# Block-sparse attention and gated FFN on one core: q turned 128 columns at a time, in a re-made order

## The chip, the core and the metric

One core of a Trainium2 chip runs the whole program. The metric is device microseconds of one execution. The engines named here are PE (TensorE: matmuls and transposes), DVE (VectorE), ACT (ScalarE), POOL (GpSimd, which here mostly issues loads that cast to bf16) and SP (SyncE, which issues the other transfers). PE writes to PSUM alone; DVE and ACT copy results from PSUM to SBUF.

## The reference

Two layers follow each other: attention with a block mask, then a feed-forward layer with a gate made by a convolution of three taps.

```python
def _attn_ref(q, k, v, sampled_blocks):          # 4 batches, 8 heads, 768 tokens, 64 wide
    ...
    scores = scale * np.matmul(q, k.transpose(0, 1, 3, 2))
    ...
    mask = np.abs(blk_i - blk_j) <= window        # blocks of 32 tokens
    mask = mask | (blk_i == 0) | (blk_j == 0) | (blk_i == n_blocks - 1) | (blk_j == n_blocks - 1)
    for qb in range(n_blocks):
        for kb in sampled_blocks[qb]:
            mask[qb * block:(qb + 1) * block, kb * block:(kb + 1) * block] = True
    ...
    return np.matmul(attn, v).astype(np.float32)  # attn: softmax over the masked scores

def _moe_ref(x, w_in, conv_w, w_out):             # 512 -> 1024 -> 512
    h = np.maximum(x @ w_in, 0.0)
    ...
    for k in range(K):
        conv_out += conv_w[k][None, None, :] * hp[:, k:k + S, :]
    gate = 1.0 / (1.0 + np.exp(-conv_out))
    return (h * gate @ w_out).astype(np.float32)
```

## The kernel before, in words

The 32 heads are taken as 16 pairs. For each pair, q and k are brought to a layout with the 64 channels on partitions: tiles `e` and `o` (five slots of each) hold the even and the odd chunks of 128 tokens, for two heads, in rows 0 to 63. Rows 64 to 87 hold the mask: on the k side a pattern of the 24 blocks, on the q side 0 or -8000 for each block, so that one matmul over 88 rows gives masked scores.

Pairs 0 to 5 are turned on PE (`kq_transposes`, from line 427), pairs 6 to 15 by transposing transfers on SP (`kq_crossbar`). For a pair on PE, `k_tr` turns k by six transposes of 128 columns into a PSUM bank `mix`, and two copies take it to `e` and `o`. q comes in two halves of 384 tokens (`g` = 0 and 1): `q_tr` (line 504) turns each half by six transposes whose weights are 64 columns wide, one for each head and chunk, into rows 0 to 63 of a `mix` bank; two `q_cp` copies, one of both heads' two chunks of one parity (512 elements) and one of the rest (256), take it on. Pair 0's first half is done head by head from fp32 loads.

The scores are made in 144 units of eight 128x128 blocks (line 742, tile `st`, two tiles of two PSUM banks each). One `exp` of 128x1024 on ACT (line 753) turns a unit into `pt` (six buffers); eight `av` matmuls of 65 columns (line 775) multiply it with v and a column of ones. When its units are done, a segment of 384 tokens is normalised (`xtok`, DVE), turned (`xT`), multiplied with `w_in` (line 864, `f1`), passed through a relu on DVE or ACT (`hE`), convolved and gated on DVE with a tanh on ACT, and multiplied with `w_out` (line 802, `f2`). Each 128 tokens of output are copied from PSUM to an `o2s` buffer (`ev`) and stored by SP (`out`). There are eight halves of a batch; the last is cut into 256 and 128 tokens, so that the end is short. The two outputs of the last segment are collected in halves of an `st` tile instead of `mix` (`tail=True`).

In the head, PE runs matmuls on a zeroed tile `warm` while the first loads land. The q side of the mask comes from six small matmuls (`w24`) on the sampled blocks into one `st` tile, three for `e` and three for `o`; two copies (`m_q0`, `m_q1`) take it to rows 64 to 87 of slot 0, and further copies spread it to the other head and slots.

Every operation is first recorded with its inputs and buffers, and then put down in the order that the string `ORDER` gives: two characters for the operation, one for the engine where there is a choice (`V` DVE, `A` ACT), and one for each buffer that it takes. Each engine works through its own instructions in that order; waits between engines are added from the tiles that instructions share. So `ORDER` decides which engine makes a copy, which buffer it takes and what stands ahead of it.

Of the kernel before, what the change touches and what calls it, by code (L numbers as in the profile page):

```python
# [20 lines left out]
000m010g0f0n0h02030410o0i0t050p0j0q0s060zA1t00k0r070AA0l081u18A1090v1F00a0b1aA0c1H20d0N0w01bA19V1c00O0xA1i11f0  # L21
1dV00yA0e1jV1l11eV1kA1gA0R1o00E4K11hA4L0D4P01nA1mV1B14Q4M01v10u0Q0P1I1wV14R14U11xV4V1T11y00G4W24Z01V34+1zV0F1AA
1W5214/30H532521p11sV05445b02715c1qV1C00I1rA4N0125g15d55h1DV4O4S1J14r1GV1281EV5i04T4X1KV25l05m134Y1LV1M05n15q14s
1NV5r1450511OV555s25610K5z05A5e0J5f5j5B35E15705F1UV20U14t1X0582j05G45J00V5K1YV31+15L51ZV5k5o5O15P1/V5p5t20V5u5Q0
5T00T5v15U26V35C05D5w5H5V16010Y614u5I155M115N6225R6500M660B05S6730C6a16b0L5W5X1636c4646f05Y26g5Z591685x06h55aV0
6o15yV6p690Z6d6e6q05+16t04v1P05/V6i6j6u6k06y16l6v14w6z160+6m06r06s6A26nV6D00S6E0X4xhW12l06F3hZ00/6I16JhX4y2m6K4
h+hYV06R06Sh/Vi316T5i4ii06W14z176Xik6wi5Ai00iji16Y04A2x11Q1i2V6/0701RAil4B6x2116B7417111SV6C75iq1290im6G762ic1
2aV47d0idir7ein7i14C2bV2z26H7j7f36L6M1is2c04DieV6U6V6Z7k46+7n06N12eV7oit2217p5722dV7s17t24V2n023V7u0737x0iu7y2q1
2oV02B02A7z1777G16O7H784E2pV2F27g0iv7h7L07926P0io4F7l2H37M7I27a7m7q7rip07v7w7A7N37B16QV17Q12rV7R7J0W7K7b07S47V0
7C07W2kV47O2sV7X57D2C4G82183107P7E17T8407cV8707FV887Uiw7Y8918c1ix2J12I7Z8d2yV0i602GV18e28h04H7+12N08i7/i7i918j3  # L30
# [12 lines left out]
lW2bZculYcn1c40lB3zlXc5c9calFVcv33Hcy03I2czb+2lUcelZlCAmg03PlVcA4cD1cfcEl+mh3Mb/cF2cjcI0ck3uV1ma1c0m23l/cJcom3
cp1cQ1cRcK5m4cw3CcxcBm5cCcGmbcS0m0m6cV0cHcLm1cM3NcWm7c+1cq1micrcX1c/m8mccscN0m9cT0cUd03d30cOd4mjcPd54cY3Zmd3+2
mkV1d81d9meV0mm03Q0da5dg03DV2mn3JV2mo3EV423OcZmfdhd1mpdi03W3Gdl1mqV3dmmy1dn1mz3/mB0mC3X0mAA0dq0mDVd2drms1mW0ds2
mtmX3Rdv1dwmYmudx3mZmE0mv40m+431d6d7mwV2mFm/dD0dbmGVdEdI1dc1n0dF4mH1n10mIdJdd2mJAmN04cde4d3dN0dK5mOn21df2dj41dO
n3dkmK1n4dP0mL494a1n5domxdpdS1dTmPVmMA4hdtdudX0dU13SV3dYdy3TVmQ1mRdZ2n6e314e4i0e4na2dzmT0nbe53mUmSVdG0e80dHe9n7
mVVdLed1dA1eeni3ea4nw1dBdMdQdRncdVef5dCdWd+ei04fndejnq0n8ek0e00eq1neer3Fd/1n9e6e744es1ev0njewnrnkex3eA1e1eb3VeB
ecnlege2nfehel4gem3YV3et0eF0nmeC4nx4ong4p2eueyen2eznheGnneK1eonyeH5eLepnonsnpeDeEeM045V4eS0eT4jnteU2eX1nuV0eYnz
eZ14bV4eI48eJnAV2eNf00mrf1eO1eP1f5146Vf23mlf6nC0eQ47nDf74nI1eR0nEVnJfd04qV0nKAfe4kV1nL0ff5nM3Ufi1nNVnvfjnF14lV  # L50
fk0eV4nnGo60eWnBfn0fonHAo8nR0fp2nSo7fs1n+1e+e/ftnTAn/nO1fu1nPo9fx0o0fyf3nQAf4o1nU0fz3fF1oafGf8f9o2nVfH4nX1oe2fg0
fK0offLo3nYogfhfP1fa0fM5flnZVfQfmfqo4frfbobfU0o5fvfcfVnWAohoA1fR0ocfwou0om3fAodfW2g01g1onfB1fIovoig21g50oog6oBop
ojfJfNfC2fOoqfSg73fTga1fDgbfXfYokfEg30org4g8olg9gj0gkgc4osoCotowgl5fZ1go1f+gpoxgq0f/gdoDoyV3gt0gugeoM0gv24mgf0oN
ggozoOoEA1oPoFgC1oQA0gDgh1gH0giA1gIoS0gE1oToV1oUV1gJ3oWgM1oXVgNp20gO4p3pe1p51pgp6p4Apfgm1gV0p7AgngrphoY0oZpigW
o+Agso/1pu0pjp0pwoG0pvp1Ag+1g/gX5oHpm2oIpnh00oJpogwh30pph4oKA2gxpxpb1h52gF0pqoLpcp80gy2pkoRgGpdAgKgzgLgPhc1prpy
hdgQpl1gY1gZhe1h1p9psh2gR1h6ptgA1hh0paAh7gShigBAhq1h80pC3hrhj3pK0pDgT1pLh9hs4gUVhf0hz0pFhgha1hkpzhl1hbVhApEhthu
pZ1hB5hv2pGp+hwhE1pHp/VhFhN0hC1hOpAhG0q31pIpBq4pJhDpMq5Aqe1hHpNhP2hJ1hm0pQ1qfhnpRpOA3qhpSqu2ho0qgpThpA2qwhI0pW0
pUA1hKqvpXpVqihL1hQhRpYAhMVpPhS0hx1hThyAq60qjhU0q01hVVq7qR0qSq8q1qTAq9qkq2AqO0qaqPqlr31qbqX1qQVqYr4qcq+0qZAqU0qd
qVq/qm3qC1qWAqor01qDqnr50qI0r1r6r80r2rd1qpri0qqr9rer7ro1qrqxrprf1qyra0qJqsqzqtrjqEqAqBqKrbqLrcrgqFrhqMA2rqqGV0qN
rrrkqHrsA1rlrtrmA3rn  # L60
# [22 lines left out]
class Graph:  # L83
# [29 lines left out]
def kernel(  # L113
# [11 lines left out]
    nc = tc.nc  # L125
# [51 lines left out]
    warm = sb.tile([128, 512], BF16, tag="warm", name="warm")  # L177
# [20 lines left out]
    def t_act(n):  # L198
        return 0.055 + n / 1200.0
# [12 lines left out]
    def T(u):  # L212
        return T0 + PACE0 * u if u < 18 else T0 + 18 * PACE0 + PACE1 * (u - 18)

    SW = 0.715
    NWARM = 11
# [4 lines left out]
    o_imem = op("ident_mem", {"DVE": 0.1}, lambda e: nc.vector.memset(ident, 0.0), -20)  # L221
    o_warm = op("warm_mem", {"DVE": 0.3}, lambda e: nc.vector.memset(warm, 0.0), -20, after=[o_imem])
    o_amem = op("a_mem", {"DVE": 0.1}, lambda e: nc.vector.memset(A, 0.0), -18, after=[o_warm])
# [4 lines left out]
    for x in range(NWARM):  # L228
        def warm_mm(e, n=512 if x < 6 else 256):
            nc.tensor.matmul(out=av_t[b_warm.index][:, 0:n], lhsT=warm[:, 0:128], rhs=warm[:, 0:n], start=True, stop=True)  # L230
        prev = op("warm", {"PE": 0.215 if x < 6 else 0.108}, warm_mm, -20 + 0.2 * x, [o_warm], after=[prev],
                  alloc=[b_warm] if x == 0 else [], uses=[] if x == 0 else [b_warm])
# [92 lines left out]
    m_q = [op("m_q0", {"ACT": 0.45, "DVE": 0.55}, q_rows(E_t[0], 0), -17, [o_w], uses=[b_w]),  # L325
           op("m_q1", {"DVE": 0.55, "ACT": 0.45}, q_rows(O_t[0], 1), -17, [o_w], uses=[b_w])]
# [96 lines left out]
    def kq_transposes(P):  # L423
# [70 lines left out]
        def q_half(g, src, ldq, nbuf, pr, hs=(0, 1)):  # L494
# [11 lines left out]
            if P == 0 and g == 1:  # L506
                pr = T(14)
# [22 lines left out]
        for hs in ([0], [1]) if P == 0 else ([0, 1],):  # L530
            q_half(0, lambda: nat_t[nb.index][:, 0, 0:384].rearrange("p (h c) -> p h c", h=2),
                   ld_q[hs[0]:hs[0] + 1] if P == 0 else ld_q, nb,
                   -16 + 2.1 * hs[0] if P == 0 else due - 3, hs)
# [6 lines left out]
        q_half(1, lambda: nq_t[nq.index], [lq1], nq, due1 - 4)  # L540
# [252 lines left out]
    def out_block(b, t, due, deps, after, tail=False):  # L793
# [13 lines left out]
        evo = op("ev", {"ACT": t_act(512), "DVE": t_dps(512) + 0.06}, lambda e: dcopy(e, o2s_t[ob.index], acc()),  # L807
                 due + 2.5, [prev], alloc=[ob], uses=[mb])
        op("out", {"SP": 0.6}, lambda e: nc.sync.dma_start(out=out[b, 128 * t:128 * t + 128, :], in_=o2s_t[ob.index]),
           due + 3, [evo], uses=[ob], dma=("hw", 0.65))  # L810
# [207 lines left out]
```

## Time and profile before

| | |
|---|---|
| time, median of 3 runs | 216.37 us (215.73 to 220.55) |
| span of the profiled execution | 213.9 us (the page gives no time beside it) |
| PE busy | 203.6 us, 95% |
| ACT busy | 193.5 us, 90% |
| DVE busy | 186.6 us, 87% |
| POOL busy | 60.4 us, 28% |
| granted TensorE clock | 1.000 |
| exps on ACT | 144, 1027 ns each |
| loads and stores | 24.81 MB, mean 116 GB/s |

The span goes from the first to the last instruction; the times of the runs include what lies around it. Matmuls overlap in PE's pipeline, so a busy share of 95% is not 95% of PE's peak: the distance from one start to the next is what a matmul costs in a dense stretch. The first exp starts at 7.88 us, and the last instruction before the final store ends at 210.9 us.

### The profile page before, as it was taken

Reading aid. Unit: us, or ns where it says so; the run is one execution under the profiler, and the core shown is the slowest. Engines: PE = TensorE matmul, PEld = TensorE weight load, DVE = VectorE, ACT = ScalarE, POOL = GpSimd, SP = SyncE. Lnnn points to the kernel's source line nnn. Section 1 sums busy time; section 2 is a strip of 40 time slices with the busy share of each in tenths; the row PEclk is TensorE's granted clock in tenths of the full one; section 3 lists DMA queues with packets and bytes.
Section 4 is the critical chain, followed back from the end, with each engine's and each line's share of the span. In section 5 each row is a group of like instructions: output and inputs, shape, how many; then the busy total and the mean of one; then the engine's idle time right before and its main releaser. Section 6 shows DMA issues by size and latency. Waiting matters only on the chain.

```text
span 213.9 us, 6829 instructions
## 1 busy us (share of the span) xinstructions
PE 203.6 (95%) x2702; PEld 154.0 (72%) x2721; DVE 186.6 (87%) x577; ACT 193.5 (90%) x252; POOL 60.4 (28%) x117
## 2 busy tenths in 40 slices
PE   7899999999999999999999999999998999999991
PEld 3679978887677775778776766787786867785740
DVE  4899989999989994999999978999799939999980
ACT  6999999999899997999999977999999988997642
POOL 8883455733323130500327152730000000000000
PEclk9999999999999999999999999999999999999999
DMA  6999898998888977693599869699941130200205
GB/s 181 186 195 202 132 123 119 113 172 99 99 123 99 138 133 162 122 106 74 103 234 96 116 104 188 105 143 114 134 154 23 20 122 3 98 5 21 80 0 196
DMA packets 48935, 24.81 MB, mean 116 GB/s; under 512 B 35120, under 2 KB 45832, under 8 KB 48904
## 3 DMA queue, kind: packets, MB, share of 16 engines
q0 software_dynamic: 19728, 11.05, 43.0%
q1 hardware_dynamic: 28888, 13.05, 30.0%
q8 instruction: 21, 0.34, 0.7%
q10 hardware_dynamic: 288, 0.30, 0.4%
q14 instruction: 10, 0.08, 0.1%
HBM read 23.08 MB, written 6.29 MB: 137 GB/s over the span
## 4 chain that ended last, share of the span: by engine, by line
PE 66%; DVE 24%; ACT 6%; issue 3%; ACTq 0%; DVEq 0%
PE st L742 19%; PE mix L802 16%; PE mix L864 12%; PE av L775 10%; DVE m L916 9%; ACT pt L753 4%; DVE m L924 4%; DVE hE L886 3%; PE st L802 2%; PE mix L504 2%; PE av L230 2%; DVE xtok L694 1%; DVE gT L971 1%; DVE o L340 1%; DVE e L340 1%
## 5 line engine op out<-in xcount | busy, mean ns | idle before, releaser
L753 ACT ACTIVATE pt<-st 128x1024 bf16<-128x1024 f32 x144 | 141.3, 1027 | 5.6 <-PE st L742 4.2
L775 PE MATMUL av<-vt,pt 128*128 128x65 bf16 x1152 | 60.4, 193 | 0.2
L775 PEld LDWEIGHTS <-pt 128*128 128x128 bf16 x1152 | 52.3, 97 | 10.1
L864 PE MATMUL mix<-xT,winb 128*128 128x384 bf16 (+2 forms) x288 | 52.8, 308 | 0.3 <-DVE hE L886 0.3
L916 DVE TENSOR_SCALAR m<-hE,cw 128x382 bf16<-128x382 bf16 (+2 forms) x192 | 49.4, 320 | 0.2
L802 PE MATMUL mix<-woutb,gT 128*128 128x512 bf16 x157 | 44.6, 379 | 1.6 <-DVE gT L971 0.6
L742 PE MATMUL st<-o 88*128 88x128 bf16 (+1 forms) x240 | 44.5, 229 | 0.3 <-ACT pt L753 0.2
L742 PE MATMUL st<-o,e 88*128 88x128 bf16 (+1 forms) x228 | 44.2, 233 | 0.2 <-ACT pt L753 0.2
L742 PE MATMUL st<-e,o 88*128 88x128 bf16 (+1 forms) x224 | 42.5, 234 | 1.2 <-ACT pt L753 1.1
L742 PE MATMUL st<-e 88*128 88x128 bf16 (+1 forms) x208 | 41.8, 239 | 0.4 <-ACT pt L753 0.2
L742 PEld LDWEIGHTS <-o 88*128 88x128 bf16 x464 | 34.3, 97 | 8.9 <-issue 2.0
L742 PEld LDWEIGHTS <-e 88*128 88x128 bf16 x436 | 32.9, 97 | 9.0 <-issue 0.9
L924 DVE TENSOR_TENSOR m<-m 128x764 bf16<-128x764 bf16 (+2 forms) x64 | 33.8, 533 | 0.3
L864 PEld LDWEIGHTS <-winb 128*128 128x128 bf16 x288 | 24.2, 97 | 8.2 <-issue 0.8
L963 ACT ACTIVATE m<-m 128x764 bf16<-128x764 bf16 (+2 forms) x32 | 26.3, 821 | 1.9 <-DVE m L924 1.8
L414 POOL COPY pace<-pt 1x1 bf16<-1x1 bf16 x24 | 7.6, 315 | 58.9 <-ACT pt L753 58.8
L802 PEld LDWEIGHTS <-gT 128*128 128x128 bf16 x192 | 15.7, 97 | 11.7 <-DVE gT L971 2.3
L886 DVE TENSOR_SCALAR hE<-mix 128x384 bf16<-128x384 f32 (+2 forms) x30 | 16.4, 553 | 7.9 <-PE mix L864 7.6
L884 ACT ACTIVATE hE<-mix 128x384 bf16<-128x384 f32 (+2 forms) x34 | 16.5, 492 | 3.1 <-PE mix L864 2.2
L971 DVE TENSOR_TENSOR gT<-m,hE 128x764 bf16<-128x764 bf16 (+3 forms) x36 | 18.3, 511 | 0.5
L694 DVE TENSOR_TENSOR xtok<-av,rcp 128x384 bf16<-128x384 f32 (+2 forms) x36 | 18.2, 507 | 0.4
L239 POOL DMA_DIRECT2D nat<-in_q_dram x23 | 16.9, 734 | 2.4 <-issue 1.9
(88 smaller groups left out, 170.0 us busy)
## 6 DMA issues: line engine op xcount, KB each, us to landing
out_dram<-o2s SPq DMA_DIRECT2D x24, 256.0 KB, 2.6
nat<-in_k_dram POOLq DMA_DIRECT2D x15, 192.0 KB, 4.0
vn<-in_v_dram POOLq DMA_DIRECT2D x15, 192.0 KB, 5.5
nat<-in_q_dram POOLq DMA_DIRECT2D x6, 192.0 KB, 4.2
winb<-in_moe_w_in_dram POOLq DMA_DIRECT2D x2, 512.0 KB, 8.4
woutb<-in_moe_w_out_dram POOLq DMA_DIRECT2D x4, 256.0 KB, 4.8
nat<-in_q_dram POOLq DMA_DIRECT2D x9, 96.0 KB, 5.4
nq<-in_q_dram POOLq DMA_DIRECT2D x6, 96.0 KB, 4.5
```

Of the source, the lines that this page charges most:

```text
L239: return op(name, {eng: occ}, lambda e: on(e).dma_start(out=dst(), in_=src), prio, deps, dma=(kind, service), **kw)
L694: nm = op("norm", {"DVE": t_dps(128 * C)}, lambda e: nc.vector.tensor_tensor(out=xtok_t[xk.index][:, 0:C].rearrange("p c h d -> p h c d"), ...
L742: nc.tensor.matmul(out=st[:, 128 * x:128 * (x + n_)], lhsT=QK[kc % 2][s][0:88, 1, hh, kc // 2, :], rhs=QK[par][s][0:88, 0, hh, idx:idx + n ...
L753: nc.scalar.activation(out=pt_t[ptb.index], in_=st_t[stb.index], func=AF.Exp, bias=0.0, scale=0.125)
L775: nc.tensor.matmul(out=o[:, off:off + 65], lhsT=pt_t[ptb.index][:, 128 * x:128 * x + 128], rhs=V_t[vslot_b[P].index][:, hh, kc, 0:65], sta ...
L802: nc.tensor.matmul(out=acc(), lhsT=gT_t[gb.index][:, ffc, 128 * t:128 * t + 128], rhs=woutb[:, ffc, :], start=(ffc == 0), stop=(ffc == NFF ...
L864: nc.tensor.matmul(out=mix_t[hb.index][:, w1 * y:w1 * y + w1], lhsT=winb[:, fc, 128 * ffc:128 * ffc + 128], rhs=xT_t[xt_buf[n].index][:, f ...
L886: nc.vector.tensor_scalar(out=dst, in0=src, scalar1=0.5, scalar2=0.0, op0=ALU.mult, op1=ALU.max)
L916: nc.vector.tensor_scalar(out=m_t[cb.index][:, x, y, 0:w], in0=hE_t[heb.index][:, f0 + y, t0 + x:t0 + x + w], scalar1=cw[:, x, f0 + y:f0 + ...
L924: nc.vector.tensor_tensor(out=m[:, a_, :, 0:w], in0=m[:, a_, :, 0:w], in1=m[:, b_, :, 0:w], op=ALU.add)
L963: th = [op("tanh", {"ACT": t_act(2 * w) + 0.04}, lambda e, cb=cb, w=w: nc.scalar.activation(out=m_t[cb.index][:, 0, :, 0:w], in_=m_t[cb.in ...
L971: nc.vector.tensor_tensor(out=gT_t[gtb.index][:, f0:f0 + 2, t0:t1], in0=m_t[cb.index][:, 0, :, 0:w], in1=hE_t[heb.index][:, f0:f0 + 2, 1 + ...
```

## The change

Five things are changed.

- For all halves of q on PE except pair 0's first, a new function `q_half` turns 128 columns at a time: the 384 columns of a partition are two heads of three chunks of 64, so that three transposes of 128 columns leave one chunk in rows 0 to 63 and the next in rows 64 to 127. Four copies, each of one head and one parity, of 256, 128, 256 and 128 elements, take them to `e` and `o`. The old function stays as `q_head` for pair 0's first half.
- `w24` becomes two operations of three matmuls each, and each mask copy names only its own.
- The tile `warm` has 256 columns, not 512, and is set to zero before `ident`. There are 14 warm matmuls of 256 columns (six of 512 and five of 256 before) and 14 more of 128, the fillers, which `ORDER` places among the first units.
- In the last segment's outputs, `ev` is two copies of 256 columns, not one of 512; `ORDER` puts the first on DVE and the second on ACT for the two outputs that use `st`.
- `ORDER` is another string, so that the place, the engine and the buffer of operations differ all over the kernel.

```diff
-    for x in range(NWARM):
-        def warm_mm(e, n=512 if x < 6 else 256):
+    for x in range(NWARM + NFILL):
+        def warm_mm(e, n=256 if x < NWARM else 128):
             nc.tensor.matmul(out=av_t[b_warm.index][:, 0:n], lhsT=warm[:, 0:128], rhs=warm[:, 0:n], start=True, stop=True)
...
-    def w24(e):
-        w = st_t[b_w.index]
-        for x, chunks in enumerate((ECH, OCH)):
+    o_w = []
+    for x, chunks in enumerate((ECH, OCH)):
+        def w24(e, x=x, chunks=chunks):
+            w = st_t[b_w.index]
             for y, (g, c) in enumerate(chunks):
...
-    o_w = op("w24", {"PE": 0.34}, w24, -17, [o_a4, o_nblk], alloc=[b_w])
+        o_w.append(op("w24", {"PE": 0.33}, w24, -17, [o_a4, o_nblk] + o_w, alloc=[] if x else [b_w], uses=[b_w] if x else []))
...
+        def q_half(g, src, ldq, nbuf, pr):
+            mb = Buf(P_mix)
+
+            def fn(e):
+                t = mix_t[mb.index].bitcast(BF16)
+                for y in range(3):
+                    nc.tensor.transpose(out=t[:, 128 * y:128 * y + 128], in_=src()[:, 128 * y:128 * y + 128], identity=ident)
...
+            X, Y = (E_t, O_t) if g == 0 else (O_t, E_t)
+            for hh, t, at, n_, p0, c0 in ((0, X, g, 2, 0, 0), (0, Y, 2 * g, 1, 64, 0), (1, X, g, 2, 64, 128), (1, Y, 2 * g, 1, 0, 256)):
+                def cp(e, hh=hh, t=t, at=at, n_=n_, p0=p0, c0=c0):
+                    dcopy(e, t[slot.index][0:64, 0, hh, at:at + n_].rearrange("p c s -> p (c s)"),
+                          mix_t[mb.index].bitcast(BF16)[p0:p0 + 64, c0:c0 + 128 * n_])
+                o = op("q_cp", {"DVE": t_d2(128 * n_) + 0.04, "ACT": t_act(128 * n_)}, cp, pr + 0.5 + 0.1 * hh, [tr], uses=[mb, slot])
...
-        evo = op("ev", {"ACT": t_act(512), "DVE": t_dps(512) + 0.06}, lambda e: dcopy(e, o2s_t[ob.index], acc()),
-                 due + 2.5, [prev], alloc=[ob], uses=[mb])
+        evo = []
+        halves = ((0, 256), (256, 512)) if tail else ((0, 512),)
+        for x, (c0, c1) in enumerate(halves):
+            evo.append(op("ev", {"ACT": t_act(c1 - c0), "DVE": t_dps(c1 - c0) + 0.06},
+                          lambda e, c0=c0, c1=c1: dcopy(e, o2s_t[ob.index][:, c0:c1], acc()[:, c0:c1]),
+                          due + 2.5, [prev], alloc=[ob] if x == 0 else [], uses=[mb] + ([ob] if x else [])))
```

More of the change, by code (lines that the diff above doesn't have):

```diff
@@ L26 @@
[L26 to L30, printed above, removed]
@@ L56 @@
[L56 to L60, printed above, removed]
+000410w0z01020D030x0y0E0K0F0G0H1N01O2100L150J0SA1G00A160I0M141qV11sA0RA05060708090a0b0c0d130e0f0g1u00B0h0N00O
@@ L176 @@
     ident24 = sb.tile([NB, NB], FP32, tag="ident24", name="ident24")
-    warm = sb.tile([128, 512], BF16, tag="warm", name="warm")
+    warm = sb.tile([128, 256], BF16, tag="warm", name="warm")
     nblk = sb.tile([NB, S], BF16, tag="nblk", name="nblk")
@@ L215 @@
     SW = 0.715
-    NWARM = 11
+    NWARM, NFILL = 14, 14
     X_PE = (0, 1, 7, 8)
     WOUT_U = (15, 19, 23, 27)
-    o_imem = op("ident_mem", {"DVE": 0.1}, lambda e: nc.vector.memset(ident, 0.0), -20)
-    o_warm = op("warm_mem", {"DVE": 0.3}, lambda e: nc.vector.memset(warm, 0.0), -20, after=[o_imem])
-    o_amem = op("a_mem", {"DVE": 0.1}, lambda e: nc.vector.memset(A, 0.0), -18, after=[o_warm])
+    o_warm = op("warm_mem", {"DVE": 0.12}, lambda e: nc.vector.memset(warm, 0.0), -20)
+    o_imem = op("ident_mem", {"DVE": 0.1}, lambda e: nc.vector.memset(ident, 0.0), -20, after=[o_warm])
+    o_amem = op("a_mem", {"DVE": 0.1}, lambda e: nc.vector.memset(A, 0.0), -18, after=[o_imem])
     o_rmem = op("r_mem", {"DVE": 0.1}, lambda e: nc.vector.memset(row23, 0.0), -18, after=[o_amem])
@@ L323, in q_rows @@
         return fn
-    m_q = [op("m_q0", {"ACT": 0.45, "DVE": 0.55}, q_rows(E_t[0], 0), -17, [o_w], uses=[b_w]),
-           op("m_q1", {"DVE": 0.55, "ACT": 0.45}, q_rows(O_t[0], 1), -17, [o_w], uses=[b_w])]
+    m_q = [op("m_q0", {"ACT": 0.45, "DVE": 0.55}, q_rows(E_t[0], 0), -17, o_w[0:1], uses=[b_w]),
+           op("m_q1", {"DVE": 0.55, "ACT": 0.45}, q_rows(O_t[0], 1), -17, o_w[1:2], uses=[b_w])]
     def k_rows(dst, x):
@@ L492, in kq_transposes, with q_head @@
                 qk_ready[(P, h, "k")] = cps
-        def q_half(g, src, ldq, nbuf, pr, hs=(0, 1)):
+        def q_head(g, src, ldq, nbuf, pr, hs=(0, 1)):
             hs, w = list(hs), len(hs)
@@ L528, in q_half @@
                 qk_ready[(P, h, g)] = cps + qk_ready[(P, h, "k")] + mask_ready[(min(s, NSLOT - 1), h)]
[L530 to L533, printed above, removed]
+        def q_half(g, src, ldq, nbuf, pr):
[4 more added lines that the diff above has]
+                    nc.tensor.transpose(out=t[:, 128 * y:128 * y + 128], in_=src()[:, 128 * y:128 * y + 128], identity=ident)
+            if P == 0:
+                pr = T(14)
+            tr = op("q_tr", {"PE": 0.168}, fn, pr, ldq + [o_ident], alloc=[mb], uses=[nbuf], after=k_trs[0:1])
+            X, Y = (E_t, O_t) if g == 0 else (O_t, E_t)
[4 more added lines that the diff above has]
+                o = op("q_cp", {"DVE": t_d2(128 * n_) + 0.04, "ACT": t_act(128 * n_)}, cp, pr + 0.5 + 0.1 * hh, [tr], uses=[mb, slot])
+                qk_ready.setdefault((P, hh, g), qk_ready[(P, hh, "k")] + mask_ready[(min(s, NSLOT - 1), hh)])
+                qk_ready[(P, hh, g)] = qk_ready[(P, hh, g)] + [o]
+        if P == 0:
+            for hs in ([0], [1]):
+                q_head(0, lambda: nat_t[nb.index][:, 0, 0:384].rearrange("p (h c) -> p h c", h=2), ld_q[hs[0]:hs[0] + 1], nb,
+                       -16 + 2.1 * hs[0], hs)
+        else:
+            q_half(0, lambda: nat_t[nb.index][:, 0, 0:384], ld_q, nb, due - 3)
         nq = Buf(P_nq)
```

80 lines of the change are left out of this document (44 added, 36 removed).

## The prediction

> **What bounds the kernel now.** I read the page first (busy shares, the chain that ended last), then busy time by stage, then the timeline of single stretches, the groups by form, and last the order of instructions on each engine, before and after, with what each waits for. The page:
>
> ```profile
> PE 203.6 (95%) x2702; PEld 154.0 (72%) x2721; DVE 186.6 (87%) x577; ACT 193.5 (90%) x252; POOL 60.4 (28%) x117
> ...
> PE 66%; DVE 24%; ACT 6%; issue 3%; ACTq 0%; DVEq 0%
> ```
>
> PE carries two thirds of the chain. That suggests that any microsecond off PE is a microsecond off the end. The stages (start:end, then busy time of PE, PEld, DVE, ACT, POOL, each with its count) say that it is not so:
>
> ```profile
> 8.00:20.00 12.00, 10.89 (x172) 8.95 (x170) 11.31 (x29) 11.76 (x14) 7.53 (x13) 1.00 1.32 195
> 20.00:40.00 20.00, 19.92 (x328) 16.79 (x326) 17.99 (x66) 19.27 (x23) 11.56 (x24) 1.00 0.92 127
> ...
> 120.00:140.00 20.00, 19.84 (x238) 14.28 (x238) 17.45 (x46) 17.11 (x21) 9.21 (x17) 1.00 0.84 131
> ```
>
> From 8 to 40 us ACT is idle for 0.24 + 0.73 = 1.0 us only, and from 8 to 180 us for 7.8 us in all. PE is the engine that ends last, but ACT, with 144 exps that start 0.92 us apart, stands just behind it.
>
> **The turn of q.** How the 64-wide and the 128-wide transposes stand in PE's timeline (start, duration, then the group):
>
> ```profile
> 13.91 0.50 PE L466 MATMUL mix<-ident,nat 128*128 128x128 bf16 x6
> 14.24 0.41 PE L775 MATMUL av<-vt,pt 128*128 128x65 bf16 x8
> ...
> 14.93 0.29 PE L775 MATMUL av<-vt,pt 128*128 128x65 bf16 x4
> 15.14 0.52 PE L504 MATMUL mix<-ident,nat 128*64 128x128 bf16 x6
> 15.60 0.23 PE L742 MATMUL st<-e,o 88*128 88x128 bf16 x1
> ```
>
> Starts, not durations, are the price. Six k transposes of 128 columns take 14.24 - 13.91 = 0.33 us, 55 ns each. Six q transposes of 64 columns take 15.60 - 15.14 = 0.46, that is 6 x 0.056 and 0.12 more, at the way out; on the way in the four av matmuls take 0.21 instead of 4 x 0.029 = 0.12, 0.09 more. So each 64-wide group pays some 0.19 to 0.21 us for the change of width alone; I take 0.19. [...]
>
> Eleven half pairs change (the first half of pairs 1 to 5, the second half of pairs 0 to 5): six transposes become three of full width. Each saves 6 x 0.056 + 0.19 - 3 x 0.055 = 0.36 us of PE, 3.9 us in all. The loads and their queues are the same.
>
> The price is in the copies. A half had two of them, of 512 and 256 elements on 64 partitions; it now has four, of 256, 128, 256 and 128:
>
> ```profile
> L340 DVE COPY e<-mix 64x512 bf16<-64x512 bf16 x5 | 2.1, 413 | 0.1
> ...
> L340 DVE COPY e<-mix 64x256 bf16<-64x256 bf16 x5 | 1.4, 279 | 0.2
> ```
>
> Doubling the elements adds 0.13 us to 0.28, so most of a copy is fixed cost. A DVE copy of 64x128 isn't in the trace: it lies between 0.07 (a 128x12 memset) and 0.28; I take 0.20, by the 128x128 copy into xT of 0.23. Start to start a half costs 0.34 + 0.25 = 0.59 before and 2 x 0.25 + 2 x 0.20 = 0.90 after: 11 x 0.31 = 3.4 us more on DVE (0.5 to 4.9 with the two ends). The new order gives some of it back: counted over the whole kernel, three relus of 384 and three evictions of 512 go from DVE to ACT. With start-to-start times of before (exp 0.92, relu 0.42, eviction 0.48 on ACT; 0.47 and 0.61 on DVE; PE by columns) the sums go, before to after: PE 191.3 to 189.9 without the 2.1 us of width changes (the turn takes off 1.85, the larger number of warm and filler matmuls adds 0.5), ACT 186.1 to 187.1, DVE 178.7 to 179.4.
>
> **The head.** The view of ACT and DVE around the first exps shows a rule of this kernel:
>
> ```profile
> 7.88 2.84 ACT L753 ACTIVATE pt<-st 128x1024 bf16<-128x1024 f32 x3
> ...
> 10.17 0.42 DVE L340 COPY e<-mix 64x512 bf16<-64x512 bf16 x1
> ...
> 10.62 0.37 ACT L336 COPY o<-mix 64x256 bf16<-64x256 bf16 x1
> ```
>
> ACT's copy from a mix bank starts when DVE's copy from the same bank ends (10.17 + 0.42): two engines never read one PSUM tile together, the second carries a wait. In the new order I follow these waits by hand. The mask's weights are ready at 4.60 as now, since their chain hangs on the same load (3.65). The query mask's six matmuls end near 5.6; DVE copies its first half to 6.2 (0.55, by the mlast cast), ACT waits and copies the second to 6.65, then q to 6.9; DVE waits for that and ends its q copy at 7.2; only then the first score matmuls go, and the first exp starts near 8.0: as now (7.88). The two-step mask is worth nothing, since the second step still follows the first.
>
> Next, ACT's second instruction is a copy of 64x128 that waits for DVE's copy from the same av bank. DVE has before that, from 7.65: o 0.36, mask 0.45, cw 0.1, the cast of v 0.75, the q copy 0.28, so it ends near 9.6; ACT copies to 9.85, and exp 2 starts there (now 8.80). ACT's next is a copy of 64x768 (0.57 to 0.86 by the rows of 64x512 and 128x768; 0.79) that waits for DVE's of the same bank, behind two mask copies: 9.6 + 0.57 + 0.56 + 0.55 = 11.3. Exp 3 starts near 12.1, against 9.72. From there ACT has nothing but exps: exp 19 starts at 12.1 + 16 x 0.92 = 26.8 at the earliest, against 25.9 now. **The head costs 0.9 us.** Bounds: 0 if the cast of v runs at the 0.27 of the other casts and both waits shrink, 2 if stage 1 meets a stall. The fillers stand where PE waits anyway; their cover is these same waits, and the eight or so behind the first scores would cost 0.06 each if it were gone.
>
> **The middle.** I counted each engine's instructions between exp 19 and exp 127, in six stages of 18 exps. Measured, the stages last 20.1, 24.3, 26.8, 23.1, 23.9, 22.3 us. The larger of PE's and ACT's sum is 18.9, 23.2, 26.2, 22.7, 23.4, 21.6 before (136.0, so 4.3 us of waits over it) and 19.6, 20.8, 23.3, 24.2, 20.9, 25.3 after (134.1). If the waits stay at 4.3, the middle gives **1.9 us**. This holds the stages apart; added up without stages, ACT's sum rises by 1.1 and PE's falls by 0.8 (and the 1 us of width changes in this part), so the bounds are 1.1 slower and 3.9 faster.
>
> **The tail.** Before (DVE's last gT, then the last evictions):
>
> ```profile
> 207.18 0.29 DVE L971 TENSOR_TENSOR gT<-m,hE 128x260 bf16<-128x260 bf16 x1
> ...
> 209.05 0.59 ACT L336 COPY o2s<-st 128x512 f32<-128x512 f32 x1 [1.19 <-PE st L802]
> 209.69 0.59 PE L802 MATMUL st<-woutb,gT 128*128 128x512 bf16 x2 [0.72 <-ACT o2s L336]
> ...
> 210.31 0.59 ACT L336 COPY o2s<-st 128x512 f32<-128x512 f32 x1 [0.68 <-PE st L802]
> ```
>
> From the last gT (207.47) to the last eviction's end (210.90) it takes 3.43 us; the transfer adds 3.0. The last matmuls wait for the eviction of the other output in the same st tile. After, the halves are one on DVE and one on ACT, and ACT's carries a wait for DVE's: one after the other, 0.42 (a 128x256 relu on DVE) and 0.39 (on ACT), 0.81 plus a handover instead of 0.59. From the last gT: four matmuls 1.05, the halves 0.47 + 0.44, four matmuls (two before) 1.08, the halves 0.47 + 0.44: 3.95. **0.5 us more**; 0.3 less if they ran side by side. PE's work from exp 127 on falls by 0.4.
>
> **The sum.** Head +0.9, middle -1.9, last stage -0.4, tail +0.5: -0.9 on a span of 213.9, so 213.0. The page gives no other time of that execution; the median of the runs (216.37) lies 2.5 above the span, and I keep that: **215.5 us**, 0.4% less.
>
> **Rivals.** *PE's saving reaches the end.* PE has 66% of the chain, and eight of its groups are q transposes. Then the 2.1 us of width changes come on top of the sum, and the re-made order halves the 4.3 us of waits: 215.5 - 2.1 - 2.1 = 211.3. For it: PE at 99.6% from 20 to 40 us. Against: ACT had 0.73 us idle there. Chance 0.27.
>
> *ACT takes over the pace, slower than before.* Place: the first 80 us, where a bank with q in it is now emptied by four copies of two engines, one after the other. In the order, 41 instructions of ACT and DVE wait for the other's read or use of the same bank, 30 before. If these waits stand in front of exps as in the head, PE's saving is hidden, ACT's added 1.1 us count in full, and head and tail stay: 216.4 + 1.1 + 0.9 + 0.5 = 218.9. It decides from the point where ACT's idle time between exps doesn't fall below the 7.8 us of now. For it: both head waits; against: DVE's copies come mostly in runs on one engine. Chance 0.25.
>
> *The turn does not pay on PE*, each group still held up by 0.2 us: 216.4 + 1.4 - 0.4 = 217.4. The k rows above (55 ns, no gap) speak against. Chance 0.03.
>
> **How the numbers follow.** The forecast has 0.45, by itself 213.5 to 217.5. 2% (4.3 us, about what a measurement of this kernel can tell from no change, since its three runs span 4.8 us) puts the bounds at 212.05 and 220.7. Faster: 0.23 of the first rival's 0.27 and 0.02 of the forecast, 0.25. Slower: 0.11 of the second's and 0.02 more, 0.13. Same: 0.62. The range reaches to both rivals: 211.2 to 219.6.
>
> **What would show it.** PE: 33 q transposes 55 ns apart, with no gap at either end. Head: first exp near 8.0, second after 9.5, third near 12; right if ACT waits for DVE there. Tail: ACT's half starting as DVE's ends, some 3.9 us from the last gT to the last eviction. Middle: exp 19 to exp 127 in 138.4 us (140.3 now), ACT at 95% or more. I am wrong if exp 3 starts before 10.5, if the middle is under 136 us (ACT was not next), or over 141 (handovers).

## The result, and the profile after

The changed kernel takes 214.81 us (median of 8 runs, 214.56 to 215.57), the one before 216.6 us on the same chip: a ratio of 0.9937 (95% interval 0.9918 to 0.9956). Three of the earlier kernel's eight runs were in a slower state (220.6 to 221.1 us); the ratio leaves them out, so it is not the quotient of the two medians. That is a real gain of 0.6%, well inside the 2% that the prediction set between "same" and "faster"; the forecast was 215.5. The profiled span is 212.7 us, 1.2 less than before (forecast 213.0).

The page of the profile after, busy time and the chain that ended last:

```profile
PE 204.0 (96%) x2705; PEld 155.0 (73%) x2705; DVE 187.9 (88%) x595; ACT 193.3 (91%) x258; POOL 60.7 (29%) x117
...
PE 73%; DVE 20%; ACT 2%; DMA 1%; issue 1%; DVEq 0%; ACTq 0%
```

Its stages (start:end, length, then the busy time of PE, PEld, DVE, ACT, POOL):

```profile
8.00:20.00 12.00, 11.55 (x159) 9.92 (x158) 10.41 (x32) 10.48 (x12) 8.65 (x15) 1.00 1.28 180
20.00:40.00 20.00, 18.87 (x318) 16.21 (x316) 19.28 (x70) 19.17 (x24) 8.30 (x18) 1.00 0.85 124
...
80.00:100.00 20.00, 20.00 (x246) 14.55 (x244) 17.55 (x51) 19.47 (x26) 3.92 (x8) 1.00 1.08 124
```

PE gained a larger share of the chain, not a smaller one. From 20 to 40 us DVE is now the busiest engine (19.28 of 20, 17.99 before) and PE waits for 1.1 us; from 80 to 195 us it stands idle for 0.2 us (2.3 before). The span cut at the places that the prediction used:

| stretch | before | after | change | forecast |
|---|---|---|---|---|
| start to exp 19 | 25.87 | 27.67 | +1.80 | +0.9 |
| exp 19 to exp 127 | 140.33 | 138.04 | -2.29 | -1.9 |
| exp 127 to the last gT's end | 41.27 | 39.84 | -1.43 | -0.4 |
| last gT to the last eviction's end | 3.43 | 4.18 | +0.75 | +0.5 |
| last transfer | 3.02 | 3.01 | 0 | 0 |

*The turn.* From the start of three q transposes to the start of the next group it takes 0.17 us, three times the 55 ns, without a gap at either end (timeline of PE):

```profile
33.65 0.33 PE L535 MATMUL mix<-ident,nq 128*128 128x128 bf16 x3
33.82 0.41 PE L795 MATMUL av<-vt,pt 128*128 128x65 bf16 x8
```

*The head.* ACT's timeline shows the three waits that were forecast, in their order, each about half a microsecond late:

```profile
8.54 1.02 ACT L773 ACTIVATE pt<-st 128x1024 bf16<-128x1024 f32 x1 [0.75 <-PE st L762]
9.94 0.26 ACT L337 COPY o<-av 64x128 bf16<-64x128 bf16 x1 [0.37 <-DVE e L341]
10.53 1.02 ACT L773 ACTIVATE pt<-st 128x1024 bf16<-128x1024 f32 x1 [0.33 <-PE st L762]
11.75 0.80 ACT L337 COPY o<-mix 64x768 bf16<-64x768 bf16 x1 [0.20 <-DVE e L341]
12.57 1.02 ACT L773 ACTIVATE pt<-st 128x1024 bf16<-128x1024 f32 x1
```

What was not forecast stands ahead of the exps: they wait for PE as well. PE's score matmuls in this stretch, after:

```profile
9.75 0.31 PE L762 MATMUL st<-o 88*128 88x128 bf16 x1
9.86 0.42 PE L762 MATMUL st<-e,o 88*128 88x256 bf16 x1
10.07 0.31 PE L762 MATMUL st<-o 88*128 88x128 bf16 x1
```

and before, at the same moment:

```profile
9.01 0.22 PE L742 MATMUL st<-o 88*128 88x128 bf16 x1
9.06 0.27 PE L742 MATMUL st<-e 88*128 88x256 bf16 x1
9.17 0.22 PE L742 MATMUL st<-o,e 88*128 88x128 bf16 x1
```

From one start to the next, 128 columns take 0.11 us after (9.75 to 9.86) and 0.05 before, 256 columns 0.21 and 0.11. TensorE runs at half rate, up to 12.4 us; the kernel before was at full rate from 5.7 us on. The granted clock of the windows doesn't say so: it reads 1.00 all through the changed kernel's head.

*The tail.* The halves of each eviction follow each other, as forecast, and the second output's matmuls start only when both halves of the first are done:

```profile
206.91 0.42 DVE L341 COPY o2s<-st 128x256 f32<-128x256 f32 x1 [1.36 <-PE st L822]
207.37 0.37 ACT L337 COPY o2s<-st 128x256 f32<-128x256 f32 x1 [0.69 <-DVE o2s L341]
...
207.79 1.02 PE L822 MATMUL st<-woutb,gT 128*128 128x512 bf16 x4
...
208.91 0.42 DVE L341 COPY o2s<-st 128x256 f32<-128x256 f32 x1 [1.57 <-PE st L822]
209.36 0.37 ACT L337 COPY o2s<-st 128x256 f32<-128x256 f32 x1 [1.01 <-DVE o2s L341]
```

### The profile page after: what moved, and what is told of

Its sections match the earlier page's. It is cut to its first block, busy times and chain, and to the rows that moved or that the text cites. A ratio compares the mean times of both kernels' runs of the same rounds, so it can differ in the third digit from the quotient of the medians.

```text
span 212.7 us, 6843 instructions
## 1 busy us (share of the span) xinstructions
PE 204.0 (96%) x2705; PEld 155.0 (73%) x2705; DVE 187.9 (88%) x595; ACT 193.3 (91%) x258; POOL 60.7 (29%) x117
## 4 chain that ended last, share of the span: by engine, by line
PE 73%; DVE 20%; ACT 2%; DMA 1%; issue 1%; DVEq 0%; ACTq 0%
PE st L762 23%; PE mix L822 18%; PE mix L888 16%; PE av L795 12%; DVE m L940 4%; DVE o L341 4%; DVE e L341 3%; DVE m L948 2%; PE st L822 2%; DVE diag L388 2%; DVE hE L910 2%; DVE xtok L714 2%; DMA o2s<-in_k_dram 1%; ACT pt L773 1%; DVE xT L341 1%
## 5 line engine op out<-in xcount | busy, mean ns | idle before, releaser
L888 PE MATMUL mix<-xT,winb 128*128 128x384 bf16 (+2 forms) x288 | 54.3, 308 | 1.2 <-DVE hE L910 0.8
L822 PE MATMUL mix<-woutb,gT 128*128 128x512 bf16 x176 | 47.1, 379 | 0.0
L762 PE MATMUL st<-o 88*128 88x128 bf16 (+1 forms) x240 | 45.1, 230 | 0.0
L762 PE MATMUL st<-e,o 88*128 88x128 bf16 (+1 forms) x224 | 43.5, 236 | 0.2
L762 PEld LDWEIGHTS <-o 88*128 88x128 bf16 x464 | 35.5, 98 | 8.1 <-issue 0.6
L762 PEld LDWEIGHTS <-e 88*128 88x128 bf16 x436 | 33.6, 98 | 8.7 <-issue 1.7
L888 PEld LDWEIGHTS <-winb 128*128 128x128 bf16 x288 | 23.5, 97 | 8.7 <-issue 1.8
L908 ACT ACTIVATE hE<-mix 128x384 bf16<-128x384 f32 (+2 forms) x39 | 18.9, 498 | 1.0 <-PE mix L888 1.0
L910 DVE TENSOR_SCALAR hE<-mix 128x384 bf16<-128x384 f32 x25 | 13.7, 553 | 3.1 <-PE mix L888 1.6
```

Of the source, the lines that this page charges most:

```text
L762: nc.tensor.matmul(out=st[:, 128 * x:128 * (x + n_)], lhsT=QK[kc % 2][s][0:88, 1, hh, kc // 2, :], rhs=QK[par][s][0:88, 0, hh, idx:idx + n ...
L822: nc.tensor.matmul(out=acc(), lhsT=gT_t[gb.index][:, ffc, 128 * t:128 * t + 128], rhs=woutb[:, ffc, :], start=(ffc == 0), stop=(ffc == NFF ...
L888: nc.tensor.matmul(out=mix_t[hb.index][:, w1 * y:w1 * y + w1], lhsT=winb[:, fc, 128 * ffc:128 * ffc + 128], rhs=xT_t[xt_buf[n].index][:, f ...
L908: nc.scalar.activation(out=dst, in_=src, func=AF.Relu, bias=0.0, scale=0.5)
L910: nc.vector.tensor_scalar(out=dst, in0=src, scalar1=0.5, scalar2=0.0, op0=ALU.mult, op1=ALU.max)
```

## The experiments

Times are medians; "ratio" is to runs of the kernel before on the same chip, with its 95% interval. The experiments ran on three chips (1, 4, 6 and 8 on one; 2, 7, 9 and the first kernel of 5 on another; 3, 10 and the second kernel of 5 on a third), so versions from different chips are better compared by ratio than by median. The questions: which part of the change made the gain, what made the head twice as long as forecast, and what the tail costs.

**1. The turn alone, in the order of before.** `q_tr` makes three transposes of 128 columns for pairs 1 to 5 and pair 0's second half, and each `q_cp` copies head by head; `ORDER` and all else stay.

```diff
+                if w == 2:
+                    s_ = src().rearrange("p h c -> p (h c)")
+                    for y in range(3):
+                        nc.tensor.transpose(out=t[:, 128 * y:128 * y + 128], in_=s_[:, 128 * y:128 * y + 128], identity=ident)
+                    return
...
+                    if w == 2:
+                        at, n_ = (g, 2) if x == 0 else (2 * g, 1)
+                        for hh, p0, c0 in (((0, 0, 0), (1, 64, 128)) if x == 0 else ((0, 64, 0), (1, 0, 256))):
+                            dcopy(e, ...)
```

> The kernel before, in its own order, with the eleven half pairs of q turned 128 columns at a time (33 transposes for 66); each q_cp becomes two copies on the engine that the order gives it. Both theories: 33 transposes 55 ns apart, no gap of 0.1 us at either end, 3.9 us less PE time. Theory A (ACT and DVE stand just behind PE, ACT has 1.0 us idle from 8 to 40 us): no more than 1 us reaches the end, 215.4 to 217, since DVE also gets 3.1 us more of copies here and no relu or eviction is taken off it. Theory B (PE paces the end): 3 us or more reaches it, 213.4 or less.

220.24 us, ratio 1.0151 (1.0094 to 1.0207), span 218.6. Both theories missed: by itself the turn made the kernel slower. This profile had TensorE at half rate up to 16.6 us, so there are two suspects: that late clock, and the copies.

**2. Four copies, narrow transposes, in the order of before.**

```diff
+                    if w == 2:
+                        at, n_ = (g, 2) if x == 0 else (2 * g, 1)
+                        for hh in hs:
+                            c0 = 256 * hh if x == 0 else 512 + 128 * hh
+                            dcopy(e, ..., m[:, c0:c0 + 128 * n_])
+                        return
```

> The kernel before, its order and its 64-column transposes unchanged, only that each half of a pair is copied out in four copies (two of 64x256, two of 64x128) where it took two (64x512 and 64x256). By the rows of the narrow turn in the new order the extra is 2 x 0.274 - 0.41 + 2 x 0.208 - 0.27 = 0.28 us a half, 3.1 us over 11 halves. Theory A, it is the copies that cost the old order its 2 us between exponentials 19 and 73: VectorE carries the chain from 37 to 60 us here too, the stages of 18 exponentials from the 19th to the 73rd take 71.1 + 1.5 to 2.5 us, and the time is 217.7 to 219. Rival B, it is the 128-column transposes (their width changes and the slow clock of the head): the stages stay within 0.5 us of 71.1 and the time is 216 to 217.

217.59 us, ratio 1.0055 (1.0024 to 1.0085), span 215.4. Between the two theories: the copies cost 1.5 us of the span, but only 0.5 of it between exps 19 and 73 (0.5 lies before exp 19, 0.5 behind exp 73).

**3. The order of before with the clock held up, with the old turn and with the new one.** To take the clock out of the comparison, both kernels got a warm run that begins with the first memset, and more full-width matmuls in the head; the ten of `fill_mm` stand behind the third group of key transposes (`ORDER` moves the first memset and places the fillers; the rest of it stays):

```diff
-        def warm_mm(e, n=512 if x < 6 else 256):
+        def warm_mm(e, n=256, r=2 if x < 6 else 4 if x == 10 else 1):
+          for _ in range(r):
...
+    def fill_mm(e):
+        for _ in range(10):
+            nc.tensor.matmul(out=av_t[0][:, 0:128], lhsT=warm[:, 0:128], rhs=warm[:, 0:128], start=True, stop=True)
```

Old turn:

> The kernel before with its clock held up in the head and nothing else: the warm run begins with the first memset (16 matmuls of 256 columns from about 1.06 us in place of 1.27), the one later warm matmul becomes four, and ten fillers of 128 columns follow the key transposes where TensorE stood still from 8.0 to 8.95 us. It is the ground for its twin with the 128-column turn. Theory A, the head of the old order depends on the moment at which TensorE comes to full rate: full rate from 5 to 6.5 us on, the 19th exponential at 25.6 to 26.4 (25.87), the time 215.6 to 216.8 with little spread. Rival B, the fillers themselves delay the head: 217 to 218.

217.14 us (215.97 to 218.91), ratio 1.0005 (0.9961 to 1.0048), span 214.1: full rate from 4.9 us on, exp 19 at 26.04. The median lies in rival B's range and the runs spread by 3 us, against theory A; but the ratio shows no cost of the fillers, and exp 19 is where theory A had it.

Wide turn:

> The old order with the 128-column turn and four copies, and the same warm run and fillers as its twin with the old turn. Theory A, the 3.4 us that the wide turn cost in the old order were mostly the half rate that TensorE had up to 16 us in those runs, which held VectorE's work of the head back into its full stretch from 20 to 60 us; the turn itself costs its copies (0.9 us by the run with four narrow copies) less what TensorE saves: full rate from 5 to 6.5 us on, the time 0 to 1.3 us above the twin's. Rival B, the wide turn itself costs it: full rate, and still 2.5 to 3.6 us above the twin. Rival C, the wide turn's saving on TensorE reaches the end of the old order: 1 to 2.5 us below the twin.

219.93 us, ratio 1.0109 (1.0066 to 1.0151), span 217.7. Full rate from 5.2 us on, and still 3.6 us of span (2.8 us of the medians) above the twin. Rival B holds, and the theory that the clock made experiment 1 slow falls. Where it goes, in the windows of the twin with the old turn first:

```profile
40.00:60.00 20.00, 19.57 (x298) 15.65 (x298) 17.99 (x55) 19.37 (x24) 8.27 (x16) 1.00 1.10 128
```

and with the wide turn:

```profile
40.00:60.00 20.00, 17.96 (x283) 14.63 (x284) 19.57 (x64) 19.05 (x23) 7.61 (x16) 1.00 1.05 124
```

PE's and DVE's busy times (first and third) have changed places: DVE is full and PE stands idle for 2 us. The chain between 36 and 60 us names ACT's exp with 35.3% for the twin, and almost only DVE here:

```profile
by line: DVE m L928 17.9%; DVE e L341 13.9%; DVE m L936 12.6%; DVE o L341 12.5%; DVE xtok L706 8.1%; DVE gT L983 6.5%; DVE m L978 4.7%; issue 4.4%; PE mix L814 4.3%; DVE diag L388 4.1%; DVE xT L341 3.3%; DVE vt L341 3.2%; DVE rcp L704 2.5%;
```

Copies into `e` and `o` (L341, those of the mask and of the pairs turned by transfers among them) are 26% of it. DVE's total rises from 186.4 to 189.4 us. Why the copies: here are two neighbouring copies of one `q_cp` and what starts behind them (timeline of DVE), with the wide turn, where the first reads rows 64 to 127 of the bank and the second rows 0 to 63:

```profile
35.28 0.46 DVE L341 COPY e<-mix 64x128 bf16<-64x128 bf16 x2 [0.43 <-ACT o L337]
35.66 0.54 DVE L928 TENSOR_SCALAR m<-hE,cw 128x382 bf16<-128x382 bf16 x2
```

and the same place in experiment 2, where all copies read rows 0 to 63:

```profile
34.74 0.35 DVE L340 COPY e<-mix 64x128 bf16<-64x128 bf16 x2 [0.31 <-ACT o L336]
35.01 0.53 DVE L922 TENSOR_SCALAR m<-hE,cw 128x382 bf16<-128x382 bf16 x2
```

The pair takes 0.38 us here from its start to the next instruction's, and 0.27 there. The single copy lasts at most some 20 ns longer. What differs is the distance between the two starts. In experiment 2 the second copy starts some 70 ns before the first has ended: 0.13 us behind the start of a 64x128 copy, 0.20 behind that of a 64x256. With the wide turn, where the second copy reads the other rows, it starts 13 to 32 ns after the end: 0.24 and 0.30 us. This holds in all 17 such pairs of DVE, and adds up to 1.75 us. The medians of these distances give, per half, 0.55 us for the two copies of the old turn (the twin), 0.66 for four that read the same rows (experiment 2) and 0.89 for the four of the wide turn: 0.11 us for their number and 0.23 for the change of rows. So the change of rows is most of the 2.3 us of span between experiment 2 and this one (215.4 to 217.7). This is read from the two traces; no run has the wide turn with its copies put in another order.

**4. The new order with narrow transposes, four copies.**

```diff
-                for y in range(3):
-                    nc.tensor.transpose(out=t[:, 128 * y:128 * y + 128], in_=src()[:, 128 * y:128 * y + 128], identity=ident)
+                for y, (hh, cc) in enumerate(((0, 0), (0, 2), (1, 0), (1, 2), (0, 1), (1, 1))):
+                    nc.tensor.transpose(out=t[0:64, 128 * y:128 * y + 128], in_=src()[:, 192 * hh + 64 * cc:192 * hh + 64 * cc + 64], identity=ident)
...
-            for hh, t, at, n_, p0, c0 in ((0, X, g, 2, 0, 0), (0, Y, 2 * g, 1, 64, 0), (1, X, g, 2, 64, 128), (1, Y, 2 * g, 1, 0, 256)):
+            for hh, t, at, n_, p0, c0 in ((0, X, g, 2, 0, 0), (0, Y, 2 * g, 1, 0, 512), (1, X, g, 2, 0, 256), (1, Y, 2 * g, 1, 0, 640)):
```

> The changed kernel, in its own order and with its four copies per half, but with 64-wide transposes (66 for 33). 3.9 us more PE time, all of it before 75 us. Theory A: PE has 2.4 us idle from 20 to 80 us in the changed kernel, so 1.0 to 1.5 us reaches the end: 215.8 to 216.3. Theory B: 3.9 us reaches it, 218.7.

215.24 us (213.92 to 215.81), ratio 0.9921 (0.9883 to 0.9959), span 212.7: below both theories, and no slower than the changed kernel as far as the intervals tell. All copies read rows 0 to 63 here, and exps 19 to 127 take 137.0 us (138.0 in the changed kernel).

**5. The new order with the whole old turn.** As 4, and the copies of both heads joined (64x512 and 64x256) at the places of the first two.

> The changed kernel's order with the turn of the kernel before: six 64-column transposes and two copies a half (64x512, 64x256), standing where the first two of the four copies stood. TensorE has some 3 us more work than in the changed kernel, VectorE some 3 us less. Theory A, the new order has room for either turn (TensorE waits 2.4 us between 20 and 80 us for VectorE in it, and these waits go when the copies shrink): 214.2 to 215.2. Rival B, the order needs TensorE's saving: 216.5 to 218. Rival C, VectorE's copies still hold the new order up: below 213.8.

215.53 us, ratio 0.9935 (0.9905 to 0.9965), a profiled span of 212.1; the time lies between theory A and rival B. The kernel without the turn has the gain of the kernel with it (0.9937; the two intervals leave room for some 0.8 us either way). **The gain is that of the new order**: the other changes touch only the head and the tail, which both got longer, and the gain lies between them. Which places of `ORDER` make it was not taken apart. Once more with the head of experiment 7:

> The new order with the old turn (six 64-column transposes and two copies a half), and the head of the run that kept the clock up; that run is its twin. Theory A, in the new order the turn is worth nothing either way, since VectorE's copies and TensorE's transposes weigh about the same: 213.5 to 214.4. Rival B, TensorE is the bound and loses 11 x 0.27 to 0.36 us, 3 to 4 us: 216 to 218. Rival C, the fewer copies win: 212 to 213.2.

214.82 us, ratio 0.9868 (0.9808 to 0.9928), between theories A and B. Its profile has the same clock as that of experiment 10 (half rate up to 10 us, exp 1 at 9.50 and 9.51), so the two can be laid side by side up to the tail: exp 19 is at 28.88 here and at 28.17 with the wide turn, exp 127 at 166.43 and 165.88. In the new order the wide turn is worth 0.7 us up to exp 19 and gives 0.15 back after it: 0.55 us, of 205.9 - 203.0 = 2.9 us that PE's busy time fell. The medians of the two, from one chip, agree: 214.82 - 213.65 = 1.2 us, of which 0.5 is experiment 10's shorter tail. It is one pair, though: this experiment's first profile, which had another clock than the changed kernel's, has exp 127 0.6 us earlier with the old turn (165.10 and 165.71).

**6. A longer warm run.** 13 warm matmuls of 320 columns and one of 256 in place of 14 of 256.

> The changed kernel with the thirteen first warm matmuls 320 columns wide instead of 256, so that PE runs without a gap until the first k transposes (3.6 to 4.3 us was a gap). If the short warm run is why matmuls up to 12.4 us were spaced at 107 ns per 128 columns: full rate from about 5.5 us on, first exp at 8.0 instead of 8.54, third at 12.1 instead of 12.57, time 0.4 to 0.8 us less if nothing later swallows it. If the clock comes late for another reason: spacing and time as in the changed kernel.

214.55 us, ratio 0.9891 (0.9834 to 0.9949), span 212.9. Full rate came at 5.8 us, but PE stood still for 1 us from 6.7 us on, and the rate fell back from 9.2 to 12.6 us; this time the granted clock (third number from the end; the row is the microsecond from 9 to 10) shows it:

```profile
9.00:10.00 1.00, 1.00 (x11) 0.82 (x9) 0.94 (x3) 0.39 (x1) 0.20 (x1) 0.61 1.41 194
```

Exp 19 starts at 27.68, as in the changed kernel: this tells nothing of what full rate is worth.

**7. The clock held up.** The warm run of 6, and fourteen more fillers; ten of them where PE stood still (`ORDER` moves that filler behind the second key transposes).

```diff
+        def warm_mm(e, n=320 if x < NWARM - 1 else 256 if x < NWARM else 128, r={20: 10, 21: 4}.get(x, 1)):
+            for _ in range(r):
...
```

> The changed kernel with a longer warm run (13 of 320 columns in place of 256) and fourteen more 128-column fillers where TensorE waits between 6.9 and 8.1 us. Theory A, the half rate of TensorE up to 12.4 us is what made the head 0.9 us longer than predicted: the matmuls are at 55 ns from about 6 us on without falling back, the third exponential starts before 12.0 (12.57), the tenth before 18.5 (19.14), and the time is 213.8 to 214.3. Rival B, the copies on VectorE and ScalarE set the head's pace whatever the clock: full rate, but the tenth exponential within 0.3 us of 19.1 and the time 214.5 to 215.0. Rival C, the clock falls back as with the longer warm run alone (9.0 to 12.4 us): 214.5 to 215.0 and nothing told.

213.91 us (213.28 to 214.77), ratio 0.9877 (0.9847 to 0.9907), span 211.9. Theory A: full rate from 4.6 us on without a fall, and the head comes out as the prediction had worked it out:

```profile
7.98 1.02 ACT L774 ACTIVATE pt<-st 128x1024 bf16<-128x1024 f32 x1 [0.38 <-PE st L763]
9.53 0.26 ACT L338 COPY o<-av 64x128 bf16<-64x128 bf16 x1 [0.53 <-DVE e L342]
9.69 1.02 ACT L774 ACTIVATE pt<-st 128x1024 bf16<-128x1024 f32 x1
11.16 0.80 ACT L338 COPY o<-mix 64x768 bf16<-64x768 bf16 x1 [0.45 <-DVE e L342]
11.98 1.94 ACT L774 ACTIVATE pt<-st 128x1024 bf16<-128x1024 f32 x2
```

Exps 1, 2, 3 and 19 start at 7.98, 9.69, 11.98 and 26.82; forecast were 8.0, 9.85, 12.1 and 26.8. It is the profile of one execution: experiment 10 and the second kernel of 5 have the same head, and there full rate came only at 10 us.

**8. The tail's evictions whole, on ACT.**

```diff
-        halves = ((0, 256), (256, 512)) if tail else ((0, 512),)
+        halves = ((0, 0), (0, 512)) if tail else ((0, 512),)
```

The empty half isn't issued; the whole one stands at the place and on the engine of the second.

> The changed kernel with the last two outputs evicted by one copy of 512 columns on ACT instead of a half on DVE and a half on ACT. If the halves run one after the other (my theory): the last gT to the last eviction's end falls from 4.17 to about 3.5 us, the time by 0.4 to 0.7 us, to 214.1 to 214.4. If they overlap or their wait is hidden: 0 to 0.3 us slower.

214.42 us, ratio 0.9884 (0.9829 to 0.9938). From the last gT to the last eviction's end 3.67 us in place of 4.18: cutting the evictions in two costs 0.5 us. The span is only 0.3 us shorter (212.5), since exp 19 came 0.5 us later in this execution.

**9. The two tail outputs in two `st` tiles.** `st_t[mb.index % 2]` with the columns from `512 * (mb.index // 2)`, where it was the other way round.

> The changed kernel with its last two outputs in two different PSUM tiles, where both had been halves of one; nothing else. Theory A, TensorE held the second output's matmuls back for the first one's eviction halves (0.42 and 0.37 us one after the other, and the matmuls start 0.05 us behind them): the second set starts at 206.9 in place of 207.79, the last eviction ends 0.7 to 0.9 us earlier, and the time is 213.9 to 214.2. Rival B, the end follows the first output's transfer or something else: 214.6 to 215.0.

214.29 us, ratio 0.9895 (0.9848 to 0.9941); 3.92 us from the last gT. The second output's matmuls now follow the ones before them without a wait:

```profile
206.38 1.03 PE L822 MATMUL mix<-woutb,gT 128*128 128x512 bf16 x4
...
207.25 1.03 PE L822 MATMUL st<-woutb,gT 128*128 128x512 bf16 x4
```

The price of the shared tile was 0.26 us; theory A had named the wait, but taken it for 0.7 to 0.9, and the time lies between the two theories.

**10. All three together.** 7, 8 and 9.

> What the runs so far favour, together: the changed kernel with the clock kept up in the head (0.8 us of the span), the last two outputs in two PSUM tiles (0.5) and each of them evicted whole by ScalarE (0.2 to 0.4). If the three add up: a span of 210.9 to 211.3 and a time of 212.7 to 213.3, clearly under both kernels. If the gain of the head is given back on the way, or the outputs' evictions queue on ScalarE behind the ones before them: 213.6 to 214.2.

213.65 us (213.43 to 214.73), ratio 0.9813 (0.9761 to 0.9865): the lowest median of all versions, and by the ratio 1.9% under the kernel before, with a wide interval; it was not run beside the changed kernel. The three did not add up to the 212.7 to 213.3 us. The tail is 3.67 us as with 8 alone, since whole evictions already let PE go on without a wait. And in the profiled execution full rate came only at 10 us: there the extra fillers run at half rate and exp 1 starts at 9.51.

## Why the prediction was right, step by step

- *The turn on PE*: 0.36 us a half, 3.9 in all, was forecast, and by the starts it is about right. With the old turn in the new order (experiment 5's second kernel) ten of the eleven groups take 0.455 us from their first start to the next group's, and 0.09 more stand ahead of them; with the wide turn (experiment 10) it is 0.165 to 0.170 and nothing: 0.38 a half, 4.2 in all. PE's busy time falls by 2.9 us only, because it counts durations, and these (0.22 us a transpose) go on over the gap of 0.15 us at the way out.
- *The copies*: a 64x128 copy was put at 0.20 and lasts 0.22; 3.4 us more on DVE were forecast. DVE's copies from `mix` of 64x128, 64x256 and 64x512 in the same two runs give 10.5 - 7.2 = 3.3 us. The sum is right, but only part of its reason, and that is luck: the prediction let each further copy pay its fixed cost again (0.31 us a half). Experiments 2 and 3 show 0.11 us a half for the number of copies; the larger part, 0.23, comes from neighbours that read different rows, a term that the prediction didn't have.
- *That the two weigh each other out* was the core of the forecast, and it holds in the new order (0.55 us for the turn). In the old order it fails: there the turn costs 3.6 us of span. The rival in which the copies make the kernel slower named the place (the first 80 us), but gave the handover of a bank between engines as the reason; the runs show DVE filled up.
- *The head*, +0.9 forecast and +1.8 measured. The step that was wrong is a term that was not there: PE's half rate up to 12.4 us. The waits of ACT for DVE, the 0.9 itself and exp 19 at 26.8 are what experiment 7 shows once PE has full rate (26.82). Why the rate rose so late isn't shown. The changed kernel's first warm matmuls end earlier, with a wait of 0.3 us ahead of the first key transposes, which the kernel before didn't have; but experiment 4 and the first kernel of 5 have the same warm run, with a wait of 0.4 and 0.2 us, and full rate came at 5.3 and 4.7 us there (to fall back at 8.7 and 8.1). The moment moves: with the same first 5 us, full rate came at 5.7 us in the kernel before and at 16.6 in experiment 1, and with the same head at 4.6 in experiment 7 and at 10 in experiment 10.
- *The fillers at no cost*: they stand in PE's waits, as said. That they could be worth something was missed (experiment 7: 0.8 us of span, with more of them). *The two-step mask* was not tried by itself.
- *The middle*: 138.4 forecast, 138.04 measured; that it is the new order's and not the turn's is borne out by 137.3 with the old turn (experiment 5) and 143.1 with the old order and the wide turn (experiment 3).
- *The last stretch*, -0.4 forecast, -1.4 measured. All versions with the new order have 39.83 or 39.84 here, with either turn, so it is the order's. Waits of PE don't explain it: its idle time from 165 to 206 us is 0.68 us before and 0.15 after, but 0.47 in experiment 10, at the same 39.84. Which step of the forecast was short stays open.
- *The tail*, +0.5 forecast, +0.75 measured: the mechanism as said, the second set of matmuls later by the wait for both halves. The 0.25 is the first set's start, 0.29 us behind the last gT (205.55 to 205.84), because PE still has another output's matmuls ahead of it; before it was 0.04.

The head (0.9 too small), the tail (0.25) and the last stretch and the middle (1.0 and 0.4 too large) nearly cancel: that the sum of -0.9 comes so near to -1.2 is in part luck. The forecast time is 0.7 above the measured one, 0.3 of it from the span and 0.4 from what lies around it: the prediction kept 2.5 us, a median of some executions less the span of another. Where a run's time and span are both on record, in every run of both kernels, the difference is 1.8 to 2.1 us.

## What to carry to other kernels

Work taken off the engine with the longest chain is worth only what the next engine lets through: here one and the same turn, 0.38 us a half off PE, gave 0.55 us in one order and cost 3.6 in the other, so a local change and a new order must be measured apart. Price copies, like matmuls, from start to start: what one copy costs depends on its neighbour (0.13 us for 64x128 behind one that reads the same rows, 0.24 behind one that reads the others; the durations are 0.20 and 0.22). In a short kernel's first microseconds, compare the distance between matmul starts with that of later stretches: half rate doesn't show in the busy share (in the changed kernel PE is busy for 4.00 of the 4 us from 8 to 12, with starts 107 ns apart for 128 columns, where later stretches have 55). And read a clock from more than one execution.

## What the chip showed that was not expected

- Half rate before the first rise is not in the granted clock (1.00 in the changed kernel's head, with starts 107 ns apart for 128 columns); a fall after it is (0.50 from 9 to 12 us in experiment 4).
- PE can be busy and stay at half rate: in experiment 1 it was busy for 7.47 of the 8 us from 8 to 16 and its rate rose only at 16.6 us, with transposes and 88-row matmuls in between. No run here separates the two.
- Where the rate fell back in the head, full rate had lasted 3.4 us and half rate lasted 3.4 us: 5.3, 8.7 and 12.1 us in experiment 4, 4.7, 8.1 and 11.5 in the first kernel of 5, 5.8, 9.2 and 12.6 in experiment 6. Ahead of each fall PE had started no matmul for 1.06 us; but in the kernel before it started none for 0.95 us from 8.0 us on, and no fall followed.
- Two neighbouring copies of DVE from PSUM overlap by some 70 ns when they read the same rows, and not at all when one reads rows 0 to 63 and the other rows 64 to 127: the second then starts 13 to 32 ns after the first has ended (17 pairs each in experiments 2 and 3).
- A copy that reads the upper 64 rows and writes the lower ones lasts longer: 293 ns in place of 278 for 64x256, and 223 in place of 216 for 64x128 (means in experiment 3's second run).
